# The first iteration of a seven-product down-projection: s4·b22 moved to fourth place in a PSUM bank of its own, s1·t1 to last, and the low parts of b22 loaded ahead of the last tiles of high parts

## The chip, the core and the metric

The kernel runs on one core of a Trainium2 chip. The time is the device time of one execution in microseconds; the number to predict is its median over several runs. In a profile, PE is TensorE's matmul side and PEld its weight loads, ACT is ScalarE, DVE is VectorE, POOL is GpSimd, SP is SyncE, whose queue issues nearly all DMAs here. The granted clock is the share of full speed that TensorE was allowed.

## What is computed

Two sequences of 4096 tokens with 640 channels go through a spectral block (a Fourier transform along the tokens, a block-diagonal complex MLP on the frequencies, a soft threshold, the inverse transform) and a gated FFN (640 to 1728 to 640). A gate per token mixes the two:

```python
g = sigmoid((x * gate_w).sum(-1, keepdims=True))
a = irfft2(softshrink(mlp(rfft2(x))))                   # block-diagonal MLP on 4 blocks of 160 channels
b = (gelu(x @ w_gate) * (x @ w_up)) @ w_down            # w_down: 1728 x 640
return g * a + (1 - g) * b
```

Everything is float32. The matmuls take each operand as a sum of a high part and a low part and add up three products of parts (high by high, low by high, high by low).

## The kernel before, in words

The program runs in three stretches. The first (to about 1380 us) computes the hidden layer of the FFN, with the forward transform's first stage in between, and writes the hidden layer to HBM (`hD`). The second (to about 1810 us) does the frequency MLP and the first stage of the inverse transform. The third has 32 iterations `i`: each takes the second stage of the inverse transform (`inv2`) for 256 tokens, in two groups of 128 rows called n1 and n2, and adds to it the down-projection of the same tokens (`down`).

**The down-projection** is a two by two block product done with seven block products in place of eight. Of the hidden layer, a11, a12, a21, a22 are blocks of 128 tokens by half of the 1728 rows; s1 to s4 are sums and differences of them, made by `h_s1` to `h_s4`. Of `w_down`, b11, b21, b22 and t1 to t4 are blocks or their sums and differences, 320 columns wide. The products are a11·b11, s2·t2, s3·t3, s1·t1, a12·b21, a22·t4 and s4·b22. The long dimension of a block is cut in seven pieces, `j` = 0 to 6. `rows` gives the matmuls of a product piece by piece: three for each j (high by high, low by high, high by low), and two at j = 6 where the left side is in `HALF`, so that a product has 21 or 20 matmuls of 128x128 by 128x320. `run` issues them into one PSUM bank in order of j. `h_op` splits a left side in its parts: the high part on ACT, the low part on DVE, into a tile `ho`.

**Iterations 1 to 31** interleave two products at a time (`duo`). **Iteration 0** does not, since the right sides are still being loaded: it runs a11·b11 (bank A), s2·t2 (B), then the 12 matmuls of `inv2(1)`, s3·t3 (C), s1·t1 (E), a12·b21 (added to A), a22·t4 (Dd), s4·b22 (added to E). After a product, DVE adds the bank to the staging tile `e` or, scaled by a gate, to the output tiles `uu`, u1 for group n1 and u2 for n2 (`scaled`). Between the products stand hooks 0 to 7, which issue what the next products need: in hook k of iteration 0 the entry of `SEQ` for k is split by `h_op`; hooks 1 and 2 load the hidden layer of iteration 1 (`h_load`, tile `hraw`), hook 2 also issues `inv2(1)`, hook 4 makes s3 and s2 of iteration 1 on POOL, hooks 5 to 7 split its a11, a22 and s2.

**The right sides** lie split in HBM (`wdf` for j = 0 to 6, `wdl` for the low parts of b22) and are loaded once into tiles `wx`, which stay for all 32 iterations. `wd_load(j, part)` issues on SP: part 0, both parts of b11 and t2; part 1, both parts of t3 and the low parts of t1 and b21; part 2, a tile with the low part of t4 and the high part of b22 (128x640; for j = 6 it comes with part 3), and, put off until `wd_later()`, a tile with the high parts of t1, b21 and t4 (128x960); part 3, the low parts of b22 for three j at a time (128x960), or for j = 6 alone (128x320), followed by the 128x640 tile of j = 6. The table `fin` says after which of the 64 steps of the second stretch (S = 64) each is issued; its last entry, S + 1, is issued just before iteration 0, and the two tiles of `wd_load(5, 2)` come in hook 0 of iteration 0.

**What sets the order.** The order is written out by hand: each engine and each queue takes its instructions in the order in which the program issues them. `st` puts a store off until `flush()`, which issues all that have gathered; a store waits on SP for the engine that writes its source, and what SP issues later stands behind it. The DMAs of SP use eight semaphores in turn, and before a DMA takes one, SP waits for the transfer that had it eight DMAs earlier. In the entry S + 1 the call `(flush,)` issues the last two stores of the inverse transform's first stage (`scr2<-is`, called `scr<-is` in the profile). Buffers of a tile pool go round, too: in iteration 0 one of the two `uu` tiles that `inv2(1)` writes takes the buffer of the `is` tile from which the first of these two stores reads, so that ACT's first write to it waits for that store to have landed.

Of the kernel before, what the change touches and what calls it, by code (L numbers as in the profile page):

```python
# [213 lines left out]
def spectral_mix_kernel(ctx: ExitStack, tc: tile.TileContext, a):  # L214
    nc = tc.nc
    out = a["out"]
# [10 lines left out]
    def bank():  # L227
        return psum.tile([P, 512], F32, name="bank", tag="bank")
# [13 lines left out]
    def small(shape, dt=F32, name="small"):  # L242
        return pool.tile(shape, dt, name=name, tag="small", bufs=18)
# [7 lines left out]
    def st(dst, src):  # L251
        late.append((dst, src))
# [217 lines left out]
    def run(dst, ops, first=True):  # L470
        for i, (l, r) in enumerate(ops):
            nc.tensor.matmul(dst, l, r, start=first and i == 0, stop=i == len(ops) - 1, skip_group_check=True)  # L472
            while inner and i == 1:
                inner.pop()()
# [669 lines left out]
    def h_s4(i):  # L1144
        d = HR[i]
        for k in range(2):
            nc.vector.tensor_sub(d["s2"][k], d["a12"][k], d["s2"][k])
        d["s4"] = d.pop("s2")
# [41 lines left out]
    def down(i, u, hooks):  # L1190
        b, na = c_seq[i]
        n1, n2 = toks(na)
        g1, g2 = gs[:, b, 1, n1:n1 + 1], gs[:, b, 1, n2:n2 + 1]
        u1, u2 = u[n1], u[n2]
        c1, c2 = slice(0, 320), slice(320, 640)
        acc = lambda: bank()[:, :320]

        def rows(a_, b_):
            h = HO.pop((i, a_))
            ops = []  # L1200
            for j, (hh, hl) in enumerate(h):
                wh, wl = WM[j][b_]
                ops.append([(hh, wh), (hh, wl)] if j == 6 and a_ in HALF else [(hh, wh), (hl, wh), (hh, wl)])
            return ops

        def blk(a_, b_):
            return sum(rows(a_, b_), [])

        def duo(X, x, Y, y, hook, more=False):

            n = [0, 0]
            hx, hy = rows(*x), rows(*y)
            tot = [sum(map(len, h)) for h in (hx, hy)]
            for j, (p, q) in enumerate(zip(hx, hy)):
                if j == 4:
                    hook()
                for k, op in ((0, p[0]), (0, p[1]), (1, q[0]), (0, p[2]), (1, q[-1]), *([(1, q[1])] if len(q) == 3 else ())):
                    nc.tensor.matmul((X, Y)[k], *op, start=n[k] == 0 and not (more and k), stop=n[k] == tot[k] - 1,  # L1218
                                     skip_group_check=True)
                    n[k] += 1  # L1220

        def scaled(dst, x, g):
            nc.vector.scalar_tensor_tensor(dst, x, g, dst, op0=OP.mult, op1=OP.add)
        hooks[0]()
        e = small([P, 2, 320], name="e")
        A = acc()
        if i:
            Dd = acc()
            duo(A, ("a11", "b11"), Dd, ("a22", "t4"), hooks[1])
            nc.scalar.activation(e[:, 0], A, AF.Copy)  # L1230
            hooks[2]()
            B, E = acc(), acc()
            duo(B, ("s2", "t2"), E, ("s1", "t1"), hooks[3])
            nc.vector.tensor_add(e[:, 0], B, e[:, 0])
            scaled(u2[:, c2], E, g2)
            hooks[4]()
            C = acc()
            duo(C, ("s3", "t3"), A, ("a12", "b21"), hooks[5], True)
            nc.vector.tensor_add(e[:, 1], C, e[:, 0])
            scaled(u2[:, c2], e[:, 1], g2)  # L1240
            scaled(u1[:, c1], A, g1)
        else:
            run(A, blk("a11", "b11"))
            nc.scalar.activation(e[:, 0], A, AF.Copy)
            hooks[1]()
            B = acc()
            run(B, blk("s2", "t2"))
            nc.vector.tensor_add(e[:, 0], B, e[:, 0])
            hooks[2]()
            C = acc()  # L1250
            run(C, blk("s3", "t3"))
            nc.vector.tensor_add(e[:, 1], C, e[:, 0])
            hooks[3]()
            E = acc()
            run(E, blk("s1", "t1"))
            for x in (E, e[:, 1]):
                scaled(u2[:, c2], x, g2)
            hooks[4]()
            run(A, blk("a12", "b21"), first=False)
            scaled(u1[:, c1], A, g1)  # L1260
            hooks[5]()
            Dd = acc()
            run(Dd, blk("a22", "t4"))
        nc.vector.tensor_add(e[:, 1], Dd, e[:, 1])
        scaled(u2[:, c1], e[:, 1], g2)
        st(out[b, n2], u2)
        hooks[6]()
        run(E, blk("s4", "b22"), first=False)
        nc.vector.tensor_add(e[:, 0], E, e[:, 0])
        scaled(u1[:, c2], e[:, 0], g1)  # L1270
        st(out[b, n1], u1)
        hooks[7]()
# [113 lines left out]
    for i, key in enumerate(keys):  # L1386
# [16 lines left out]
        for j, t in enumerate(quads):  # L1403
            def hook(k):
                for f in slots.get((i, 7 * j + k), ()):
                    f()
# [27 lines left out]
    S = len(steps)  # L1434
# [3 lines left out]
    for ch in range(1, 2 * NCH):  # L1438
        b, c = chunks[ch]
# [6 lines left out]
    def events(i, j):  # L1446
        for f, *args in todo.get((i, j), []):
            f(*args)
    wl = lambda part, *js: [(wd_load, j, part) for j in js]
# [9 lines left out]
           S - 2: [(h_load, 0, 0), *wl(1, 2), (h_load, 0, 1)],  # L1459
           S - 1: [(c_split, 0), (h_op, 0, "a11"), *wl(1, 3, 4, 5), *wl(0, 6), (h_s3, 0, nc.gpsimd), (c_load, 1)],  # L1460
           S: [(h_s2, 0), (h_op, 0, "s2"), (c_split, 1)],
           S + 1: [*wl(1, 6), (flush,), *wl(2, 6), (wd_later,), *wl(2, 4), (wd_later,), *wl(3, 0, 3, 6), (h_s1, 0)]}
    for i in range(S + 2):
        events(i, 0)
        flush()
# [16 lines left out]
        if 0 <= i - 1 < S:  # L1482
            b, c, n = steps[i - 1]
# [5 lines left out]
            f(*args)  # L1489


    SEQ = dict(enumerate(("s3", "s1", "a12", "a22", "s4")))
    DUO = {0: "s1", 2: "s3", 3: "a12", 4: "s4"}
    for i in range(len(c_seq)):
        n = i + 1 if i + 1 < len(c_seq) else None
# [3 lines left out]
        def step(k):  # L1499
            def f():  # L1500
# [7 lines left out]
                if k == (1 if i else 0):  # L1508
                    h_s4(i)
                op = (SEQ if i == 0 else DUO).get(k)  # L1510
                if op:
                    h_op(i, op)
                if n is not None:
# [16 lines left out]
                    if k == 7:  # L1530
                        h_op(n, "s2")
            return f
        down(i, uu, [step(k) for k in range(8)])
    flush()

# [20 lines left out]
```

## Time and profile before

| | |
|---|---|
| median of 3 runs | 2548.75 us (2548.2 to 2549.05) |
| the profiled execution: its own time, its span | 2548.73 us, 2547.0 us |
| granted clock over the span | 0.998 |
| PE busy | 2533.7 us, 99% of the span |
| DVE, ACT, POOL busy | 2053.1, 1491.7, 372.4 us |
| HBM read and written | 300.55 MB and 179.64 MB |
| matmuls of the down-projection: iteration 0 and the last 20 (line 472); the rest (line 1218) | 764; 3844 |

A row of the timeline has the start in us from the span's start, the duration, engine, line, operation, output and inputs, the count of merged instructions, and in brackets the idle time of the engine before it with what ended it. A row of the waits has the total, the number of times and the longest. A row of the chain has start, duration and what ran or was under way. A row of the windows has the stretch and its length, the busy time and the count of instructions of PE, PEld, DVE, ACT and POOL in it, TensorE's granted clock, the busy share of the DMA engines and the GB/s that they moved.

### The profile page before, as it was taken

To read this page: it belongs to the slowest core of one execution; us is meant where nothing else is said; L and a number is where in the kernel's file an instruction comes from. 1 tells how busy PE (TensorE), PEld (TensorE's weight loads), DVE (VectorE), ACT (ScalarE), POOL (GpSimd) and SP (SyncE) were. 2 spreads that over 40 slices of the span, in tenths; PEclk is the share of its full clock that TensorE was granted. 3 is DMA by queue.
4 is the path that set the end of the run, shared out by engine and by line. 5 is a ranking of instruction groups with operands and counts; after the bars stand their busy time and mean duration, and the time that the engine had idled before them with its cause. 6 is when DMAs were issued, how large, how long until landed. Compare 5 with 4: busy or idle time off the path is not lost.

```text
span 2547.0 us, 54577 instructions
## 1 busy us (share of the span) xinstructions
PE 2533.7 (99%) x20317; PEld 2529.6 (99%) x20317; DVE 2053.1 (81%) x4214; ACT 1491.7 (59%) x3489; POOL 372.4 (15%) x379
## 2 busy tenths in 40 slices
PE   9999999999999999999999999999899999999999
PEld 9999999999999999999999999999899999999999
DVE  7778767777777766776667788888899999899998
ACT  5555555666665655565556787777544444444443
POOL 0000000000000000000003111111133333333332
PEclk9999999999999999999999999999999999999999
DMA  6565647676767667776677455548744444444432
GB/s 222 188 226 187 220 169 230 201 243 209 223 207 249 199 221 231 224 227 214 213 226 228 127 153 156 155 145 266 267 145 152 156 146 143 137 152 156 153 131 100
DMA packets 345311, 483.77 MB, mean 190 GB/s; under 512 B 24717, under 2 KB 220941, under 8 KB 345045
## 3 DMA queue, kind: packets, MB, share of 16 engines
q1 hardware_dynamic: 330212, 438.47, 53.8%
q0 software_dynamic: 14832, 41.82, 4.6%
q8 instruction: 160, 2.62, 0.4%
q14 instruction: 107, 0.87, 0.1%
HBM read 300.55 MB, written 179.64 MB: 189 GB/s over the span
## 4 chain that ended last, share of the span: by engine, by line
PE 98%; DMA 1%; DVE 1%; ACT 0%; issue 0%; SPq 0%; DVEq 0%; ACTq 0%
PE bank L472 56%; PE bank L1218 22%; PE bank L295 14%; PE bank L798 3%; PE bank L632 1%; PE bank L879 1%; PE bank L880 1%; DMA wx<-wdf 1%; DMA s<-scr 0%; PE bank L881 0%; PE bank L1310 0%; DVE xd L430 0%; DVE xo L279 0%; DVE h L543 0%; DVE w L279 0%
## 5 line engine op out<-in xcount | busy, mean ns | idle before, releaser
L472 PE MATMUL bank<-xo,w 128*128 128x256 f32 x11736 | 1360.4, 277 | 0.3 <-ACT u L498 0.3
L472 PEld LDWEIGHTS bank<-xo,w 128*128 128x128 f32 x11736 | 1351.8, 188 | 0.8 <-ACT u L498 0.7
L1218 PE MATMUL bank<-wx,ho 128*128 128x320 f32 x3844 | 560.8, 306 | 0.0
L1218 PEld LDWEIGHTS bank<-wx,ho 128*128 128x128 f32 x3844 | 557.2, 188 | 0.0
L498 ACT ACTIVATE u<-bank 128x256 f32<-128x256 f32 x408 | 156.6, 384 | 255.9 <-PE bank L472 250.0
L279 DVE TENSOR_TENSOR ho<-hraw,ho 128x640 fp32r<-128x640 f32 (+3 forms) x384 | 272.1, 749 | 22.6 <-ACT ho L276 19.7
L276 ACT ACTIVATE ho<-hraw 128x640 fp32r<-128x640 f32 x320 | 167.1, 571 | 98.2 <-PE bank L1218 65.8
L498 ACT ACTIVATE p<-bank 128x256 f32<-128x256 f32 x204 | 78.6, 385 | 151.0 <-PE bank L472 63.4
L279 DVE TENSOR_TENSOR xo<-xraw,xo 128x512 fp32r<-128x512 f32 x209 | 143.3, 686 | 24.2 <-ACT xo L276 23.7
L531 DVE TENSOR_TENSOR u<-bank,u 128x256 f32<-128x256 f32 x204 | 86.0, 422 | 89.6 <-ACT u L498 86.8
L279 DVE TENSOR_TENSOR xs<-xr,xs 64x640 fp32r<-64x640 f32 x128 | 105.0, 820 | 57.5 <-ACT xs L276 55.5
L295 PE MATMUL bank<-wm,h 128*128 128x320 f32 (+1 forms) x792 | 137.6, 309 | 0.0
L276 ACT ACTIVATE xo<-xraw 128x512 fp32r<-128x512 f32 x208 | 130.4, 627 | 7.1 <-DMA xraw<-in_xT_dram 5.2
L540 DVE TENSOR_TENSOR u<-bank,u 128x256 f32<-128x256 f32 x204 | 85.6, 419 | 60.4 <-PE bank L472 59.5
L634 DVE TENSOR_TENSOR as<-bank,as 64x320 f32<-64x320 f32 x256 | 113.9, 484 | 24.9 <-ACT as L633 23.8
L472 PE MATMUL bank<-wx,ho 128*128 128x320 f32 x764 | 119.5, 312 | 6.6 <-DMA wx<-wdf 6.6
L472 PEld LDWEIGHTS bank<-wx,ho 128*128 128x128 f32 x764 | 114.7, 192 | 7.1 <-issue 5.2
L295 PEld LDWEIGHTS bank<-wm,h 128*128 128x128 f32 (+1 forms) x792 | 117.9, 185 | 1.3
L585 POOL MEMSET h<- 64x512 f32 x16 | 8.4, 523 | 748.2 <-PE bank L632 408.4
L514 DVE TENSOR_TENSOR p<-bank,p 128x256 f32<-128x256 f32 x204 | 86.6, 425 | 37.1 <-PE bank L472 32.7
L276 ACT ACTIVATE ho<-hs 128x640 fp32r<-128x640 f32 (+1 forms) x128 | 68.9, 570 | 68.0 <-DVE ho L279 50.8
L633 ACT ACTIVATE as<-bank 64x320 f32<-64x320 f32 x256 | 96.8, 427 | 16.4 <-PE bank L632 13.9
(167 smaller groups left out, 3658.9 us busy)
## 6 DMA issues: line engine op xcount, KB each, us to landing
xo<-xD SPq DMA_DIRECT2D x124, 512.0 KB
xraw<-in_xT_dram SPq DMA_DIRECT2D x225, 256.0 KB
hD<-h SPq DMA_DIRECT2D x224, 256.0 KB
hraw<-hD SPq DMA_DIRECT2D x128, 320.0 KB
xD<-xo POOLq DMA_DIRECT2D x64, 512.0 KB, 4.1
sc<-scr SPq DMA_DIRECT2D x65, 320.0 KB
xr<-in_x_dram SPq DMA_DIRECT2D x64, 320.0 KB
scr<-as SPq DMA_DIRECT2D x64, 320.0 KB
```

What stands on the lines that cost most here:

```text
L276: nc.scalar.activation(dst, src, AF.Copy, scale=scale)
L279: eng.tensor_sub(dst, src, hi.bitcast(F32))
L295: nc.tensor.matmul(dst, l, r, start=i == 0, stop=i == len(ops) - 1)
L472: nc.tensor.matmul(dst, l, r, start=first and i == 0, stop=i == len(ops) - 1, skip_group_check=True)
L498: copy = lambda d, s_: nc.scalar.activation(d, s_, AF.Copy)
L514: nc.vector.tensor_add(p1, A, p1)
L531: nc.vector.tensor_add(u4, C, u4)
L540: nc.vector.tensor_add(u2, C, u2)
L633: nc.scalar.activation(stg[hi, cs], pa[lo, :320], AF.Copy)
L634: nc.vector.tensor_add(stg[hi, cs], pa[hi, :320], stg[hi, cs])
L798: nc.tensor.matmul(pz[:, kp * P:(kp + 1) * P], SC[b, c, kp][:, o:o + P], ft, start=True, stop=True)
L1218: nc.tensor.matmul((X, Y)[k], *op, start=n[k] == 0 and not (more and k), stop=n[k] == tot[k] - 1, skip_group_check=True)
```

## The change

Iteration 0 gets a new order: s4·b22 runs fourth, into a bank F of its own, and s1·t1 runs last, into E. `SEQ` follows, so hook 1 splits s4 and hook 4 splits s1. Since E no longer gathers two products, DVE adds it to u1 and to u2 apart, and `e` is added to the outputs as soon as s3·t3 is done. In the entry S + 1 of `fin`, part 3 (`wdl`, and the last 128x640 tile) is issued right after part 1 of j = 6, ahead of the stores of `flush` and of part 2 of j = 6 and 4.

```diff
             nc.vector.tensor_add(e[:, 1], C, e[:, 0])
+            for u_, c_, x, g in ((u2, c2, 1, g2), (u2, c1, 1, g2), (u1, c2, 0, g1)):
+                scaled(u_[:, c_], e[:, x], g)
             hooks[3]()
-            E = acc()
-            run(E, blk("s1", "t1"))
-            for x in (E, e[:, 1]):
-                scaled(u2[:, c2], x, g2)
+            F = acc()
+            run(F, blk("s4", "b22"))
+            scaled(u1[:, c2], F, g1)
             hooks[4]()
             run(A, blk("a12", "b21"), first=False)
             scaled(u1[:, c1], A, g1)
             hooks[5]()
             Dd = acc()
             run(Dd, blk("a22", "t4"))
+            scaled(u2[:, c1], Dd, g2)
+            hooks[6]()
+            E = acc()
+            run(E, blk("s1", "t1"))
+            scaled(u1[:, c2], E, g1)
+            st(out[b, n1], u1)
+            scaled(u2[:, c2], E, g2)
+            st(out[b, n2], u2)
+            hooks[7]()
+            return
...
-           S + 1: [*wl(1, 6), (flush,), *wl(2, 6), (wd_later,), *wl(2, 4), (wd_later,), *wl(3, 0, 3, 6), (h_s1, 0)]}
+           S + 1: [*wl(1, 6), *wl(3, 0, 3, 6), (flush,), *wl(2, 6), (wd_later,), *wl(2, 4), (wd_later,), (h_s1, 0)]}
...
-    SEQ = dict(enumerate(("s3", "s1", "a12", "a22", "s4")))
+    SEQ = dict(enumerate(("s3", "s4", "a12", "a22", "s1")))
```

On SP, between the second stretch and iteration 0, the one piece of the difference (`wdf_111` is j = 6, `wdf_109` j = 4, `wdf_110` j = 5; the first row is part 1 of j = 6, the last two are issued in hook 0):

```order
 L1068 DMA wx<-wdf_111 128x1280
+L1068 DMA wx<-wdl 128x960 x2
+L1068 DMA wx<-wdl 128x320
+L1068 DMA wx<-wdf_111 128x640
 L256 DMA scr_1_71<-is 16x16x320 x2
 L1068 DMA wx<-wdf_111 128x960
 L1068 DMA wx<-wdf_109 128x640
 L1068 DMA wx<-wdf_109 128x960
-L1068 DMA wx<-wdl 128x960 x2
-L1068 DMA wx<-wdl 128x320
-L1068 DMA wx<-wdf_111 128x640
 L1068 DMA wx<-wdf_110 128x640
```

Four loads move from behind the two stores and three loads to ahead of them.

On PE, the fourth product of iteration 0 from j = 3 on, before (s1·t1 into E; `wx_26620`, `wx_26633`, `wx_26616` are the 128x960 tiles of j = 4, 5 and 6, the other tiles are part 1):

```order
L472 MATMUL bank_26779<-wx_26620,ho_26668 128x320 x2
L472 MATMUL bank_26779<-wx_26490,ho_26668 128x320
L472 MATMUL bank_26779<-wx_26633,ho_26669 128x320
L472 MATMUL bank_26779<-wx_26633,ho_26670 128x320
L472 MATMUL bank_26779<-wx_26492,ho_26669 128x320
L472 MATMUL bank_26779<-wx_26616,ho_26669 128x320
```

and now (s4·b22 into F; `wx_26625`, `wx_26631` are the 128x640 tiles of j = 4 and 5, `wx_26616` the low parts for j = 3 to 5, `wx_26618` both parts for j = 6):

```order
L472 MATMUL bank_26783<-wx_26616,ho_26668 128x320
L472 MATMUL bank_26783<-wx_26625,ho_26668 128x320 x2
L472 MATMUL bank_26783<-wx_26616,ho_26668 128x320
L472 MATMUL bank_26783<-wx_26631,ho_26669 128x320
L472 MATMUL bank_26783<-wx_26631,ho_26670 128x320
L472 MATMUL bank_26783<-wx_26616,ho_26669 128x320
L472 MATMUL bank_26783<-wx_26618,ho_26669 128x320 x2
```

The fourth product no longer reads the 128x960 tiles of high parts; of j = 4 and 5 it reads the 128x640 tiles, each of which is issued just ahead of the 128x960 tile of the same j.

## The prediction

> **What bounds the kernel now.** I read the waits of PE first, then PE's timeline where iteration 0 stands, then SP's timeline and the DMA windows there, to see what PE waits for. PE is busy for 99% of the span. Its whole list of waits (total, times, longest) has one row that concerns this change:
>
> ```profile
> PE bank L472 <- DMA wx<-wdf: 6.6, 2, 4.9
> ```
>
> Both pauses lie in iteration 0 (start, duration, idle time before it in brackets):
>
> ```profile
> 1809.89 6.32 PE L472 MATMUL bank<-wx,ho 128*128 128x320 f32 x42
> 1816.05 1.90 PE L295 MATMUL bank<-s2s,v 128*128 128x320 f32 x12
> 1817.79 5.04 PE L472 MATMUL bank<-wx,ho 128*128 128x320 f32 x33
> 1824.49 0.70 PE L472 MATMUL bank<-wx,ho 128*128 128x320 f32 x3 [1.66 <-DMA wx<-wdf]
> 1830.13 12.45 PE L472 MATMUL bank<-wx,ho 128*128 128x320 f32 x66 [4.93 <-DMA wx<-wdf]
> 1842.41 17.87 PE L1218 MATMUL bank<-wx,ho 128*128 128x320 f32 x122
> ```
>
> The 33 matmuls are the 21 of s3·t3 and the first 12 of s1·t1, j = 0 to 3. Then PE waits 1.66 us for the high part of t1 at j = 4, does its three matmuls, and waits 4.93 us for j = 5. The last row gives the undisturbed pace, 17.87 / 122 = 0.1465 us a matmul. At that pace the 66 would take 9.67 us; they took 12.45, so 2.78 us are lost once more. The windows (stretch, length, PE busy, the other engines, clock, DMA share, GB/s) show why:
>
> ```profile
> 1822.21:1825.62 3.41, 1.32 (x8) 0.81 (x6) 2.19 (x6) 0.23 (x1) 0.00 (x0) 1.00 1.03 413
> 1825.63:1829.04 3.41, 0.00 (x0) 0.00 (x0) 0.00 (x0) 0.00 (x0) 0.00 (x0) 0.50 1.04 409
> 1829.04:1832.45 3.41, 2.32 (x9) 2.35 (x10) 0.34 (x1) 1.08 (x2) 0.35 (x1) 0.50 1.05 379
> 1832.45:1835.86 3.41, 3.41 (x14) 3.41 (x14) 3.37 (x4) 0.07 (x1) 3.41 (x3) 0.50 0.14 46
> 1835.87:1839.00 3.13, 3.13 (x23) 3.13 (x23) 3.07 (x5) 1.05 (x2) 1.57 (x2) 1.00 0.00 0
> ```
>
> The clock fell to half at 1825.63, at the end of a stretch in which PE was busy for 1.32 of 3.41 us, and came back 10.24 us later, after a stretch busy throughout. So the stall costs 1.66 + 4.93 + 2.78 = 9.37 us. That is all that this change can win.
>
> Why the tiles are late stands in SP's timeline, in its row of waits on DVE, and in the chain (start, duration from issue to landing):
>
> ```profile
> 1804.19 1.26 SPq L256 DMA_DIRECT2D scr<-is  x2
> 1806.17 0.33 SPq L1068 DMA_DIRECT2D wx<-wdf  x1
> 1814.62 1.21 SPq L256 DMA_DIRECT2D scr<-is  x2
> 1815.87 1.84 SPq L1068 DMA_DIRECT2D wx<-wdf  x3
> 1817.77 2.24 SPq L1068 DMA_DIRECT2D wx<-wdl  x3
> 1820.06 2.79 SPq L1068 DMA_DIRECT2D wx<-wdf  x3
> ...
> SPq L256 <- DVE is L976: 68.2, 13, 8.2
> ...
> 1803.46 8.88 DMA s<-scr
> 1815.87 6.59 DMA wx<-wdf
> 1822.53 7.46 DMA wx<-wdf
> ```
>
> From 1806.5 to 1814.6 SP issues nothing: it stands at the flush, 8.2 us, until DVE has written the last `is`. Nine loads queue behind. Meanwhile the DMA engines use up what was issued before:
>
> ```profile
> 1810.00:1812.00 2.00, 2.00 (x16) 2.00 (x15) 1.25 (x3) 1.17 (x3) 0.00 (x0) 1.00 1.05 396
> 1812.00:1814.00 2.00, 2.00 (x16) 2.00 (x15) 1.63 (x4) 1.77 (x6) 0.00 (x0) 1.00 0.97 380
> 1814.00:1816.00 2.00, 2.00 (x16) 2.00 (x15) 2.00 (x6) 1.74 (x5) 0.00 (x0) 1.00 0.18 65
> 1816.00:1818.00 2.00, 2.00 (x16) 1.94 (x15) 2.00 (x5) 0.91 (x3) 0.00 (x0) 1.00 1.06 312
> 1818.00:1820.00 2.00, 2.00 (x15) 2.00 (x15) 2.00 (x5) 2.00 (x5) 0.00 (x0) 1.00 0.90 241
> 1820.00:1822.00 2.00, 2.00 (x16) 2.00 (x15) 2.00 (x5) 2.00 (x5) 0.00 (x0) 1.00 0.94 326
> 1822.00:1824.00 2.00, 0.83 (x6) 0.58 (x4) 1.94 (x6) 0.44 (x2) 0.00 (x0) 1.00 1.01 414
> ```
>
> A full queue moves 380 to 414 GB/s; I take 400, or 0.4 MB a us. From 1814 the queue runs dry, 65 GB/s, and the next three rows refill slowly. Against 400 the four rows miss 335 + 88 + 159 + 74 = 656 GB/s over 2 us, 1.31 MB, or 3.3 us.
>
> **The change part by part: the loads.** A 128x960 tile is 0.492 MB, a 128x640 tile or a store 0.328 MB, the short `wdl` load 0.164 MB, the 128x1280 tile 0.655 MB. I reckon SP's transfers as moved in the order of their issue, and need one anchor: the second `s<-scr` landed at 1803.46 + 8.88 = 1812.34, and behind it stood two stores and the 128x1280 tile of 1806.17, 1.31 MB, 3.28 us: it lands at 1815.6. As a check on the kernel before: the two stores and the nine loads behind it, to the tile of 1822.53, are 4.26 MB, 10.65 us, so 1826.3 with a full queue; it landed at 1822.53 + 7.46 = 1829.99. The 3.7 us between are the 3.3 us of the dry queue, near enough.
>
> Now the four moved loads, 1.475 MB, come ahead of the flush. Two things could hold them on SP, a buffer and a semaphore. By the order with its waits they wait for four transfers only, the last being the first `s<-scr`, which the second one's 1812.34 bounds; so they are issued before the queue runs out at 1815.6, and the flush is not later than its 1814.62. The queue stays full. With 1815.6 and 0.4 MB a us: the four loads have landed at 1819.3, the stores at 1820.9, the 128x960 tile of j = 6 at 1822.2, the 128x640 tile of j = 4 at 1823.0, its 128x960 tile at 1824.2, the 128x640 tile of j = 5 at 1825.0, its 128x960 tile at 1826.3.
>
> **The products.** All up to s3·t3 stays, so the fourth product starts at 1817.79 + 21 x 0.1465 = 1820.87. It is now s4·b22. It wants the low parts from 1821.2 (there since 1819.3), the 128x640 tile of j = 4 at 1820.87 + 12 x 0.1465 = 1822.63 and that of j = 5 three matmuls later. These land at 1823.0 and 1825.0: stalls of 0.4 and 1.6 us, 2.0 in all. With 380 or 420 GB/s the second is there at 1825.5 or 1824.6, so 1.5 to 2.5 us. a12·b21 then starts at 1825.8 and wants the last tile, of j = 5, at 1828.0; it is there at 1826.3. s1·t1, which made both waits, comes 20 + 20 matmuls later still.
>
> The Trainium skill speaks against this reckoning: "DMA: Bandwidth & Descriptors", section Specifications, gives a limit of about 358 GB/s from HBM for a core. By it the stall would be 3.0 us and the sum 1 us higher; the rows above, up to 414 GB/s, do not agree, and I stay with them.
>
> **The engines.** These rows of ACT, DVE and POOL stand around it:
>
> ```profile
> 1817.87 1.78 ACT L1185 ACTIVATE uu<-bank,gs 128x320 f32<-128x320 f32 x4 [1.09 <-PE bank L295]
> 1819.52 1.99 ACT L276 ACTIVATE ho<-hraw 128x640 fp32r<-128x640 f32 x4
> 1830.88 0.74 ACT L276 ACTIVATE ho<-hraw 128x640 fp32r<-128x640 f32 x1 [8.43 <-DMA hraw<-hD]
> 1817.02 2.22 DVE L279 TENSOR_TENSOR ho<-hraw,ho 128x640 fp32r<-128x640 f32 x4
> 1821.39 1.33 DVE L279 TENSOR_TENSOR ho<-hraw,ho 128x640 fp32r<-128x640 f32 x3
> 1832.11 0.55 DVE L1223 SCALAR_TENSOR_TENSOR uu<-bank,gs,uu 128x320 f32<-128x320 f32 x1 [7.61 <-PE bank L472]
> 1834.56 2.89 POOL L1136 TENSOR_TENSOR hs<-hraw 128x640 f32<-128x640 f32 x2
> ```
>
> Splitting s4 in place of s1 is one small DVE subtraction more (a third where 2.22 has four): done near 1819.4, wanted at 1820.9. The three additions of `e` after s3·t3 cost 3 x 0.55 us, and DVE has one instruction more than before; both lie under the stall and under 8 us of products, and would cost 1 to 2 us only if DVE had to feed a12 or a22 at once. The bank F is free without a wait that the order shows. The second `uu` tile on ACT waits for the first store, due at 1820.1: then three of its four writes (1.34 us), the two high parts of a12 (1.0) and DVE's 1.33 end at 1823.8; PE wants a12 at 1825.8, and would at 1823.8 without the stall. That store's cover is thus 2.0 us. Iteration 1 wants its first left sides at 1835.0, 7.4 us sooner than 1842.41; `hraw`, 1830.88 before, lands 3.7 us sooner with the queue and is split while a22·t4 and s1·t1 run, and POOL's sums, which end at 1837.45 before the change, are wanted only 41 matmuls, 6 us, after that start. I put all of this at nothing.
>
> **The sum**, on the profiled execution's 2548.73 us: less 1.66, 4.93 and 2.78, plus 2.0: 2541.4 us, with 1.5 to 2.5 us of stall 2540.9 to 2541.9. The median of the runs, 2548.75, is the same to 0.02 us, so nothing is added for it.
>
> **The rivals.**
>
> A shorter stall. If the 128x640 tiles land a us or more earlier than reckoned, 0 to 1 us is left: 2539.4 to 2540.4. The slow refill has no row that says how early loads behave under stores; against it stands the steady 400.
>
> The clock falls all the same. The row of 1822.21 shows a fall after 39% busy in 3.41 us; 2.0 us of stall in the same length leaves 41%, if one such stretch holds all of it, and more if two share it. No row shows where between 39% and a busy stretch the limit lies. Once fallen, the rows show the clock back only after a stretch of 3.41 us wholly busy, so 3.4 to 6.8 us at half pace cost 1.7 to 3.4 us: 2543.1 to 2544.8.
>
> The Trainium skill, "TensorE: Matmul & The Clock Gate", section "What's actually happening", has half rate return after at least one idle window of about 3.4 us. By that rule the stall leaves the clock alone, and the sum stays. The trace agrees in the length but not in "idle": the longest pause before the fall was 1.66 us, then 0.44 us of the next.
>
> The queue refills no better. If the slow rows 1816 to 1822 came from the stores among the loads and not from the dry queue, and the gap at 1814 reappears later, the last tile still lands at 1829.99 and the 128x640 tile of j = 5, now just ahead of it, at 1828.8. Then s4·b22 waits 5.7 us in place of 6.6, with the same clock: 2547.8. For it speaks that two stores lie in the slow rows; against, that stores moved at 380 to 396 GB/s at 1810 to 1814.
>
> Slower: the store holds ACT. The two stores now have 1.475 MB of loads ahead of them, and ACT's `uu` waits for the first. Were its packets put off until the queue is empty, all loads and the 1.83 MB of `hraw` first, it would land near 1830.9; a12 would be ready 3.7 us later, at 1834.6, which makes 8.8 us of waiting after the 2.0, and with 2.78 of clock the total is 4.2 us over before: 2552.9. It decides from a landing at about 1826.7. Against it: the stores of 1804.19 stood in a full queue too, and by the row of 1814 nothing was left in it.
>
> **How the numbers follow.** A measurement of this kernel can tell about 0.2%, 5.1 us, from no change. The forecast, a short stall at full clock, 2541.4: 0.48. Shorter stall: 0.08. Clock falls: 0.30, of which 0.19 below 2543.65 (the 0.2% line). Queue no better: 0.10. Store holds ACT: 0.04, about half beyond the line on the slow side, with other mishaps. Faster 0.48 + 0.08 + 0.19 = 0.75; slower 0.03; same 0.22. The range leaves out the last two cases: from 2539.0, where nothing of the 9.37 us is left, with the spread of the runs, to 2545.5, above the fallen clock.
>
> **What would show it.** Right: SP issues three `wx<-wdl` between 1807 and 1813; no window from 1814 to 1822 below 350 GB/s; PE idle about 2 us near 1823 to 1825, on `wx<-wdf`, none before a12·b21 or s1·t1; 66 or so matmuls at 0.1465 us and PEclk 1.00. Wrong: `wx<-wdl` issued after 1814.6; a pause of PE that ACT or DVE ends; a row of half clock; a pause before iteration 1.

## The result and the profile after

The changed kernel takes 2542.65 us, the median of 10 runs (2540.69 to 2543.53); the kernel before, on the same chip, 2548.44 us (10 runs, 2547.04 to 2549.73). The ratio is 0.9976, 95% interval 0.9966 to 0.9985. The profiled execution of after took 2543.41 us, with a span of 2541.6.

PE's timeline of after around iteration 0 (start, duration, idle time before it in brackets):

```profile
1810.23 6.31 PE L472 MATMUL bank<-wx,ho 128*128 128x320 f32 x42
1818.12 4.97 PE L472 MATMUL bank<-wx,ho 128*128 128x320 f32 x33
1823.86 0.70 PE L472 MATMUL bank<-wx,ho 128*128 128x320 f32 x3 [0.77 <-DMA wx<-wdf]
1825.93 11.33 PE L472 MATMUL bank<-wx,ho 128*128 128x320 f32 x66 [1.37 <-DMA wx<-wdf]
1837.10 13.10 PE L1218 MATMUL bank<-wx,ho 128*128 128x320 f32 x89
```

The two pauses are now in s4·b22, 0.77 and 1.37 us where before had 1.66 and 4.93. The next 66 matmuls take 11.33 us, which is 1.66 more than 66 x 0.1465. From the first matmul of iteration 0 to the first of iteration 1 are 1837.10 - 1810.23 = 26.87 us; in before these are 1842.41 - 1809.89 = 32.52. This stretch, **iteration 0** below, is what the profiles are compared by: it holds the pauses that the change is about, and not what differs between runs ahead of it. Behind it, from the first matmul of iteration 1 to the end of the span, nearly all profiles of this document have 704.4 to 704.6 us; the two exceptions are named where they come up.

SP's timeline of after:

```profile
1807.60 3.65 SPq L1068 DMA_DIRECT2D wx<-wdl  x3
1811.79 0.32 SPq L1068 DMA_DIRECT2D wx<-wdf  x1
1814.85 1.50 SPq L256 DMA_DIRECT2D scr<-is  x2
1816.45 3.52 SPq L1068 DMA_DIRECT2D wx<-wdf  x5
```

The DMA windows of after there (the last number is GB/s, the third from the end the clock):

```profile
1814.00:1816.00 2.00, 2.00 (x16) 2.00 (x15) 2.00 (x5) 1.67 (x5) 0.00 (x0) 1.00 1.02 413
1816.00:1818.00 2.00, 2.00 (x16) 2.00 (x15) 2.00 (x5) 1.00 (x2) 0.00 (x0) 1.00 1.03 406
1818.00:1820.00 2.00, 2.00 (x15) 2.00 (x15) 1.94 (x6) 0.58 (x2) 0.00 (x0) 1.00 1.07 403
1820.00:1822.00 2.00, 2.00 (x16) 2.00 (x15) 0.94 (x3) 0.90 (x3) 0.00 (x0) 1.00 1.02 411
```

The flush still waits for DVE, until 1814.85, but four loads have been issued ahead of it, and the four windows that had 65, 312, 241 and 326 GB/s now have 403 to 413.

The windows of the clock in after:

```profile
1822.35:1825.76 3.41, 1.44 (x9) 0.92 (x7) 3.31 (x8) 2.91 (x7) 0.00 (x0) 1.00 1.03 407
1825.77:1829.18 3.41, 3.25 (x12) 3.28 (x13) 3.35 (x8) 1.04 (x2) 0.08 (x1) 0.50 1.07 390
1829.18:1832.59 3.41, 3.41 (x25) 3.41 (x24) 1.49 (x3) 1.05 (x2) 3.41 (x3) 1.00 0.22 73
```

One stretch of 3.41 us holds nearly all of both pauses, 1.97 of 2.14 us, with PE busy for 1.44 of it, 42%; the clock is at half for the 3.41 us behind it.

ACT's timeline of after shows how the store holds it up:

```profile
1821.10 1.37 ACT L1185 ACTIVATE uu<-bank,gs 128x320 f32<-128x320 f32 x3 [2.44 <-DMA scr<-is]
```

ACT stands still for 2.44 us, until the store has landed. No row of PE names ACT or DVE here.

### The profile page after: what moved, and what is told of

Its sections match the earlier page's. It is cut to its first block, busy times and chain, and to the rows that moved or that the text cites. A ratio compares the mean times of both kernels' runs of the same rounds, so it can differ in the third digit from the quotient of the medians.

```text
span 2541.6 us, 54579 instructions
## 1 busy us (share of the span) xinstructions
PE 2533.0 (100%) x20317; PEld 2529.0 (100%) x20317; DVE 2053.7 (81%) x4215; ACT 1491.8 (59%) x3489; POOL 372.3 (15%) x379
## 4 chain that ended last, share of the span: by engine, by line
PE 97%; DVE 1%; DMA 1%; issue 0%; ACT 0%; DVEq 0%
PE bank L472 55%; PE bank L1218 22%; PE bank L295 14%; PE bank L798 3%; PE bank L632 1%; DMA wx<-wdf 1%; PE bank L879 1%; PE bank L880 1%; DMA wx<-wdl 0%; PE bank L881 0%; PE bank L1321 0%; DVE xd L430 0%; DVE xo L279 0%; DVE wl L728 0%; DVE h L543 0%
```

## The experiments

The theory: the tiles are late because the DMA queue runs dry at the flush, and the clock falls in the stretch that holds PE's pauses. The main rivals: the new order of products makes the gain by itself; the order among the loads does, and the flush is no matter; the store's hold on ACT reaches PE. Each kernel was timed beside before on its chip; after itself was timed twice more, as after_again and after_third.

| kernel | median (runs), us | ratio to before, 95% | iteration 0 in its profile, us |
|---|---|---|---|
| before | 2548.44, 2547.87, 2548.23, 2547.39 | | 32.52 |
| after | 2542.65 (10) | 0.9976 [0.9966, 0.9985] | 26.87 |
| loads_only | 2544.23 (11) | 0.9986 [0.9978, 0.9995] | 27.52 |
| order_only | 2545.38 (11) | 0.9988 [0.9979, 0.9996] | 28.12 |
| behind_flush | 2547.73 (11) | 0.9997 [0.9988, 1.0006] | 30.01 |
| filled | 2540.92 (7) | 0.9974 [0.9963, 0.9985] | 25.19 |
| after_again | 2542.24 (10) | 0.9979 [0.9970, 0.9988] | 25.21 |
| small_ahead | 2540.19 (6) | 0.9969 [0.9958, 0.9981] | 22.75 |
| high_ahead | 2542.10 (7) | 0.9973 [0.9962, 0.9984] | 23.07 |
| a12_early | 2541.09 (11) | 0.9977 [0.9968, 0.9986] | 24.81 |
| after_third | 2541.08 (11) | 0.9977 [0.9968, 0.9986] | 24.70 |
| filled_again | 2541.41 (11) | 0.9977 [0.9969, 0.9986] | 25.06 |
| small_ahead_again | 2539.55 (5) | 0.9969 [0.9956, 0.9981] | 23.01 |
| small_ahead_a12 | 2538.49 (5) | 0.9966 [0.9954, 0.9979] | 23.80 |

The four medians of before belong to the four groups in the table's order: after; loads_only to filled; after_again to a12_early; after_third to small_ahead_a12.

### The loads alone

The kernel before with after's place of the loads; the order of products stays that of before:

```diff
-           S + 1: [*wl(1, 6), (flush,), *wl(2, 6), (wd_later,), *wl(2, 4), (wd_later,), *wl(3, 0, 3, 6), (h_s1, 0)]}
+           S + 1: [*wl(1, 6), *wl(3, 0, 3, 6), (flush,), *wl(2, 6), (wd_later,), *wl(2, 4), (wd_later,), (h_s1, 0)]}
```

> The loads of after (three wx<-wdl and one wx<-wdf ahead of the flush) with the order of products of before (s1*t1 fourth, s4*b22 last). Queue theory (a tile's landing is set by the bytes ahead of it in a queue that stays full): s1*t1 wants the 128x960 tiles of j = 4 and 5 near 1823.0 and 0.44 us behind; after's trace has them landing near 1825.0 and 1827.0, so two pauses of 2.0 and 1.5 us, 3.5 in all in place of 6.6. With the clock at half for 3.4 to 6.8 us besides: 2548.7 - 9.4 + 3.5 + (1.7 to 3.4) = 2544.5 to 2546.2; with the clock left alone 2542.8. Rival, that the whole gain comes from the order of products: 2548.5, as before. Rival, that it all comes from the loads: 2542.6, as after.

PE's timeline of loads_only:

```profile
1824.30 0.69 PE L472 MATMUL bank<-wx,ho 128*128 128x320 f32 x3 [1.54 <-DMA wx<-wdf]
1826.36 11.19 PE L472 MATMUL bank<-wx,ho 128*128 128x320 f32 x66 [1.37 <-DMA wx<-wdf]
1837.39 0.90 PE L1218 MATMUL bank<-wx,ho 128*128 128x320 f32 x5
1838.61 17.49 PE L1218 MATMUL bank<-wx,ho 128*128 128x320 f32 x119 [0.32 <-DVE ho L279]
```

Pauses of 1.54 and 1.37 us in place of 1.66 and 4.93, and a clock at half for 3.41 us. The median, 2544.23, is 0.3 us below the range expected with a fall of the clock. So the loads win 3.6 us of the median by themselves, and the rival that the whole gain comes from the order of products is out. The rival that it all comes from the loads is not excluded by the medians, since the two intervals overlap from 0.9978 to 0.9985; against it stand the pauses, 2.91 us in all where after has 2.14, and the next kernel. The last row has a pause that after does not have: in iteration 1 PE waits 0.32 us for a split by DVE. From iteration 1 to the end this profile has 705.1 us.

### The order of products alone

```diff
-           S + 1: [*wl(1, 6), *wl(3, 0, 3, 6), (flush,), *wl(2, 6), (wd_later,), *wl(2, 4), (wd_later,), (h_s1, 0)]}
+           S + 1: [*wl(1, 6), (flush,), *wl(2, 6), (wd_later,), *wl(2, 4), (wd_later,), *wl(3, 0, 3, 6), (h_s1, 0)]}
```

> The order of products of after with the loads of before (three wx<-wdl behind the flush, last but three in the queue). Queue theory: s4*b22 then waits for wx<-wdl (landing 1825.7 to 1827.3 in before) and for the 128x640 tile of j = 5 (1828.8 in before), wanted at 1823.1: 5.7 us of pause in one or several pieces in place of 6.6, and the half clock as in before: 2547.5 to 2548.5. Rival, that the order of products alone makes the gain: 2541 to 2543.

PE's timeline of order_only:

```profile
1817.72 3.53 PE L472 MATMUL bank<-wx,ho 128*128 128x320 f32 x23
1824.32 2.77 PE L472 MATMUL bank<-wx,ho 128*128 128x320 f32 x13 [3.06 <-DMA wx<-wdl]
1827.59 10.53 PE L472 MATMUL bank<-wx,ho 128*128 128x320 f32 x66 [0.50 <-DMA wx<-wdf]
1837.95 18.08 PE L1218 MATMUL bank<-wx,ho 128*128 128x320 f32 x124
```

My number missed: 2545.38, about 2 us below the range, though still 3 us above after. The waits are the ones expected, but they are 3.56 us in all and not 5.7: the first `wx<-wdl` is there at 1824.3, where before's had 1825.7. Of this 1.4 us the flush itself gives 0.6 (it issues at 1813.99, in before at 1814.62); the rest is open. And with matmuls between the two pauses PE is busy for 2.90 of the 3.41 us behind the fall of the clock, so it is at half for 3.41 us, not 10.24. The order alone is thus worth 2.5 us of the median (its interval ends at 0.9996, just short of no change) and is no mere preparation for the loads. One part wins 3.6, the other 2.5, both 5.8 to 6.3.

### The moved loads right behind the flush

```diff
-           S + 1: [*wl(1, 6), *wl(3, 0, 3, 6), (flush,), *wl(2, 6), (wd_later,), *wl(2, 4), (wd_later,), (h_s1, 0)]}
+           S + 1: [*wl(1, 6), (flush,), *wl(3, 0, 3, 6), *wl(2, 6), (wd_later,), *wl(2, 4), (wd_later,), (h_s1, 0)]}
```

> After with one edit: the four moved loads stand right behind the flush, in the same order among all other loads, so that the queue has nothing between about 1814 and 1815.6, as in before. Theory of the dry queue: the window 1814 to 1816 is again below 150 GB/s, the 128x640 tile of j = 5 lands near 1828.8, s4*b22 waits about 5.7 us, the clock falls: 2547.5 to 2548.5. Rival, that the order among the loads is what matters and the flush is not: 2542.0 to 2543.5, as after.

In this profile iteration 0 begins at 1812.61, 2.7 us later than in before. Its DMA windows:

```profile
1816.00:1818.00 2.00, 2.00 (x15) 2.00 (x15) 2.00 (x6) 2.00 (x6) 0.00 (x0) 1.00 0.39 158
1818.00:1820.00 2.00, 2.00 (x16) 2.00 (x15) 2.00 (x5) 0.67 (x2) 0.00 (x0) 1.00 0.68 188
1820.00:1822.00 2.00, 2.00 (x15) 1.93 (x14) 1.97 (x5) 1.98 (x6) 0.00 (x0) 1.00 1.04 296
1822.00:1824.00 2.00, 2.00 (x15) 1.84 (x13) 1.97 (x6) 2.00 (x5) 0.00 (x0) 1.00 1.02 353
```

And PE's timeline of behind_flush:

```profile
1812.61 6.32 PE L472 MATMUL bank<-wx,ho 128*128 128x320 f32 x42
1828.79 1.17 PE L472 MATMUL bank<-wx,ho 128*128 128x320 f32 x3 [2.70 <-DMA wx<-wdf]
1830.85 11.93 PE L472 MATMUL bank<-wx,ho 128*128 128x320 f32 x66 [0.90 <-DMA wx<-wdf]
1842.62 17.64 PE L1218 MATMUL bank<-wx,ho 128*128 128x320 f32 x121
```

The dry spot is back, and the gain is gone by the median: 2547.73, where before has 2547.87. By iteration 0 more than half of it is gone: 30.01 us, between after's 26.87 and before's 32.52. From after this kernel differs only in four loads that stand on the other side of the flush, in the same order among all loads, so the rival "order among the loads" can't be the cause of after's gain. That order does count, though: order_only has the same four loads behind the three others of the entry S + 1 in place of ahead of them, and is 2.3 us shorter by the median (the intervals overlap, 0.9979 to 0.9996 and 0.9988 to 1.0006) and 1.9 us shorter in iteration 0. In both kernels the windows right behind the dry spot refill slowly, as in before; why is open. The pauses are 3.84 us, with a short one of 0.24 on `wx<-wdl`. The matmuls between them are slowed by the half clock, and the row of j = 5 starts at 1830.85, 18.2 us behind the start of iteration 0, where before's rows, undisturbed, put it 13.2 behind: 5.1 us late of the 5.7 expected. The clock is at half for 6.83 us.

### PE kept busy in the pauses

14 matmuls more, into a bank that a22·t4 later starts anew; what is computed stays:

```diff
-            F = acc()
-            run(F, blk("s4", "b22"))
+            F, Dd = acc(), acc()
+            x, y = HO[i, "s4"][0][0], WM[0]["b11"][0]
+            for j, r in enumerate(rows("s4", "b22")):
+                for k in range({4: 5, 5: 9}.get(j, 0)):
+                    nc.tensor.matmul(Dd, x, y, start=True, stop=True, skip_group_check=True)
+                for k, (l, m) in enumerate(r):
+                    nc.tensor.matmul(F, l, m, start=j == 0 and k == 0, stop=j == 6 and k == 1, skip_group_check=True)
...
-            Dd = acc()
```

> After with 14 matmuls more in s4*b22, 5 ahead of its row j = 4 and 9 ahead of j = 5; they write into the bank that a22*t4 uses later and starts anew, so what is computed stays. They stand in the two pauses (0.77 and 1.37 us in the profile of after), so PE is busy there. Clock theory (the runs of after, 2540.7 to 2543.5, differ by whether the clock falls after these pauses): the clock stays at 1.00, the 14 matmuls take the place of 2.05 us of pause, and all runs lie at 2541.0 to 2541.9. Rival, that the spread has another source: the same spread, median 2542.6. If the 14 matmuls do not fit in the pauses, up to 1 us more than 2541.4.

PE's timeline of filled, where L1260 is the added line:

```profile
1822.13 0.89 PE L1260 MATMUL bank<-wx,ho 128*128 128x320 f32 x5
1822.87 0.72 PE L1262 MATMUL bank<-wx,ho 128*128 128x320 f32 x3
1823.43 1.48 PE L1260 MATMUL bank<-wx,ho 128*128 128x320 f32 x9
```

No pause is left and the clock stays at 1.00. Six of seven runs lie at 2540.56 to 2541.64, one at 2544.41 with a mean clock of 1.000, so that no fall made it long. Beside after on one chip, though:

> After with the 14 filling matmuls, beside after on one chip. Clock theory: no run at a mean clock of 0.999 or below, median 2540.6 to 2541.4, 0.5 to 2 us below after_third. Rival: no difference from after_third.

> After itself, unchanged, timed beside the three kernels that follow. 2540.7 to 2543.5 as before; by the clock theory its runs fall into two groups, near 2541 without a fall of the clock and near 2543 with one.

> After itself beside filled_again and the two kernels with the small tiles ahead. Median 2541.5 to 2543, runs from 2540.7 to 2546; where a profile shows the stretch of 3.41 us that holds the pauses busy 42% or less, the clock falls and the run is 1.5 to 2 us longer; where it is busy 60% or more, it does not.

filled_again has 2541.41, after_third 2541.08: no gain, and one of its 11 runs has a mean clock of 0.999. The reason is in the profiles of after_again and after_third, where the clock stays up behind PE's pauses as they are. The stretch ahead of the long pause and the one that holds it, of after_again:

```profile
1820.72:1824.13 3.41, 3.38 (x24) 3.10 (x22) 3.16 (x8) 3.26 (x8) 0.00 (x0) 1.00 1.03 398
1824.13:1827.54 3.41, 2.08 (x15) 1.86 (x14) 3.30 (x8) 0.89 (x2) 0.00 (x0) 1.00 1.04 395
```

and of after_third:

```profile
1821.06:1824.47 3.41, 3.33 (x23) 3.08 (x23) 2.86 (x7) 2.89 (x7) 0.00 (x0) 1.00 1.03 412
1824.47:1827.88 3.41, 2.05 (x13) 1.82 (x14) 3.31 (x8) 1.26 (x4) 0.00 (x0) 1.00 1.04 404
```

The long pause is there, 1.33 and 1.36 us, and PE is busy for 61% and 60% of the stretch that holds it. But the short one, 0.77 us in after, is all but gone: the first rows leave PE idle for 0.03 and 0.08 us. In both the next stretch is at 1.00, and iteration 0 is 25.21 and 24.70 us, not 26.87. So what decides between these three profiles is first the short pause, that is, how soon the 128x640 tile of j = 4 lands against PE's need of it; whether the same two pauses would leave the clock up if the stretches began elsewhere, no profile shows.

How often the clock falls in after's runs can only be bounded. All profiles here with a fall in iteration 0 have a mean clock of 0.998 or 0.999, all without it 1.000; by that, at most 8 of after's 31 runs had a fall (2542.36 to 2545.85) and at least 23 had none. It is a bound, since the clock also falls behind PE's last matmuls: in after_again it is at half for the last 2.3 us of the span, which by itself nearly makes a 0.999. So the clock theory holds for the profiles, and fell as an explanation of the whole spread: runs without a fall reach 2544.47.

### The store's hold on ACT

```diff
-                if (i, k) == (0, 2):
-                    ahead.update(inv2(1))
                 if k in (0, 5):
                     flush()
                 if k == (1 if i else 0):
                     h_s4(i)
                 op = (SEQ if i == 0 else DUO).get(k)
                 if op:
                     h_op(i, op)
+                if (i, k) == (0, 2):
+                    ahead.update(inv2(1))
```

> After, with the split of a12 written ahead of the second pair of uu tiles, so that ACT makes it before it stands 2.44 us for the store scr<-is. Prediction's step: the store's hold on ACT is covered by the products, so the time stays that of after within 0.3 us (median 2541.5 to 2543.0), and the pauses in s4*b22 stay. Rival, that the hold reaches PE by a way that the trace does not name: 1 to 2.4 us less.

The median is 2541.09, 1.15 us below after_again's 2542.24 on the same chip. That lies in the rival's range, but the intervals overlap almost wholly, after_third without this edit has the same ratio, and iteration 0 of 24.81 us stands between after_third's 24.70 and after_again's 25.21. PE still waits, on `wx` alone:

```profile
1822.85 0.72 PE L472 MATMUL bank<-wx,ho 128*128 128x320 f32 x3 [0.19 <-DMA wx<-wdf]
1824.90 9.85 PE L472 MATMUL bank<-wx,ho 128*128 128x320 f32 x66 [1.33 <-DMA wx<-wdf]
```

So the hold is covered as far as the trace tells. A gain of some tenths can't be told from none.

### More tiles ahead of the flush

small_ahead moves both 128x640 tiles that s4·b22 waits for ahead of the flush too:

```diff
-           S + 1: [*wl(1, 6), *wl(3, 0, 3, 6), (flush,), *wl(2, 6), (wd_later,), *wl(2, 4), (wd_later,), (h_s1, 0)]}
+           S + 1: [*wl(1, 6), *wl(3, 0, 3, 6), *wl(2, 4, 5, 6), (flush,), (wd_later,), (h_s1, 0)]}
...
-                if (i, k) == (0, 0):
-                    wd_load(5, 2)
-                    wd_later()
```

> After, with the two 128x640 tiles of j = 4 and 5 moved ahead of the flush as well, and the 128x960 tiles in the order 4, 5, 6 behind the stores. Queue theory, with 0.4 MB a us from the tile of after that lands at 1816.7: the 128x640 tiles are there near 1821.0 and 1821.8, 1.9 and 1.6 us before s4*b22 wants them, so its two pauses (2.14 us) go; a12*b21 starts 2.1 us sooner and wants the 128x960 tiles from 1826.0 on; they land near 1824.7, 1825.9 and 1827.1, so 0 to 0.5 us of pause there. Without a pause of 1 us the clock stays up: 2543.4 - 2.1 - 1.7 + (0 to 0.5) = 2539.6 to 2540.1, median of the runs 2539.5 to 2540.5. Rival, that the pause only moves into a12*b21 (the same bytes are ahead of the last tile): 1 us or more there, 2541 to 2543.

> Both 128x640 tiles of j = 4 and 5 ahead of the flush, beside after on one chip. Queue theory: no pause of PE on wx in iteration 0, median 2539.0 to 2540.5, 1.5 to 3 us below after_third. Rival, that the runs at 2541 to 2542 of the first trial are its usual time: 0 to 1 us below after_third.

PE's timeline of small_ahead:

```profile
1810.00 6.32 PE L472 MATMUL bank<-wx,ho 128*128 128x320 f32 x42
1817.89 15.02 PE L472 MATMUL bank<-wx,ho 128*128 128x320 f32 x102
1832.75 18.07 PE L1218 MATMUL bank<-wx,ho 128*128 128x320 f32 x124
```

From s3·t3 on, all 102 matmuls of iteration 0 run in one piece, 0.147 us each. 2540.19 and 2539.55: the second is 1.5 us below after_third on one chip, with runs of 2537.94 to 2540.41 against 2539.85 to 2543.59; the intervals of the two ratios overlap, so the size is rough. That the pauses are gone is plain in both profiles. The pause does not move into a12·b21. That the bytes ahead of the last tile are the same is no harm, since that tile is wanted later.

high_ahead does the like for the order of products of before: the 128x640 and 128x960 tiles of j = 4 to 6 ahead of the flush, the low parts behind it. The difference is against before:

```diff
-           S + 1: [*wl(1, 6), (flush,), *wl(2, 6), (wd_later,), *wl(2, 4), (wd_later,), *wl(3, 0, 3, 6), (h_s1, 0)]}
+           S + 1: [*wl(1, 6), *wl(2, 6), (wd_later,), *wl(2, 4), (wd_later,), *wl(2, 5), (wd_later,), (flush,), *wl(3, 0, 3, 6), (h_s1, 0)]}
...
-                if (i, k) == (0, 0):
-                    wd_load(5, 2)
-                    wd_later()
```

> The order of products of before (s1*t1 fourth, s4*b22 last), with all 128x640 and 128x960 tiles of j = 4 to 6 ahead of the flush and the three wx<-wdl and their 128x640 tile behind it. Queue theory: only what stands ahead of the flush counts, not which product comes fourth. The 128x960 tiles of j = 4 and 5 land near 1820.8 and 1822.8, wanted at 1823.0 and 1823.4; wx<-wdl and its 128x640 tile near 1827, wanted after 1829. No pause, clock at 1.00: 2539.4 to 2540.5. Rival, that s4*b22 fourth is needed for the gain: 2542.5 or more, as loads_only (2544.2).

PE's timeline of high_ahead:

```profile
1810.65 6.32 PE L472 MATMUL bank<-wx,ho 128*128 128x320 f32 x42
1818.54 15.34 PE L472 MATMUL bank<-wx,ho 128*128 128x320 f32 x102
1833.72 0.90 PE L1218 MATMUL bank<-wx,ho 128*128 128x320 f32 x5
1834.86 17.49 PE L1218 MATMUL bank<-wx,ho 128*128 128x320 f32 x119 [0.25 <-DVE ho L279]
```

The mechanism is confirmed: no pause in iteration 0 with s1·t1 fourth either. The time is not: three runs lie at 2538.36 to 2540.52, four at 2542.10 to 2542.32, all at a mean clock of 1.000, and the median is near after_again's. As in loads_only, PE waits a little for a split by DVE in iteration 1, 0.25 us, and from there to the end the profile has 705.0 us. The profile is of one of the short runs, so what the four others lose stays open.

The last kernel adds the earlier splits to small_ahead (a12 as in a12_early, and the step of a22 ahead of the additions of `e`):

> small_ahead with the splits of a12 and a22 written earlier (a12 ahead of the second pair of uu tiles, a22 ahead of the additions of e). small_ahead shows no pause on ho in iteration 0, so the time should be that of small_ahead_again within 0.4 us; a gain of 1 us would mean a wait on ACT or DVE that the profile of small_ahead did not show.

Its five runs are 2538.34 to 2539.69, median 2538.49, the lowest of all, 8.9 us below before on its chip. That is 1.1 us under small_ahead_again, more than the 0.4 expected, but the two ratios' intervals overlap almost wholly, and its profile has a pause of 0.76 us on a split by DVE that small_ahead's two profiles do not have. All five runs are shorter than the shortest of after_third's 11, 2539.85. That it beats before and after is shown; that it beats small_ahead is not.

## Why the prediction was right, and where not

**The dry queue: right.** SP issues the `wx<-wdl` loads at 1807.60 to 1811.25, within the 1807 to 1813 named, and all windows of after from 1814 to 1822 are above 350 GB/s (after_again has one of 347). behind_flush undoes this alone and loses the gain of the median. The reckoning took the slow refill behind the dry spot as part of it, and after bears that out, but why the refill is slow no run shows.

**The stall: right in place and cause, its sum partly by luck.** In the profiled execution it is 0.77 + 1.37 = 2.14 us against 0.4 + 1.6 = 2.0, in s4·b22, for `wx<-wdf`, with none ahead of a12·b21 or s1·t1. In the other two profiles of after it is 1.36 and 1.43 us, below the range of 1.5 to 2.5: the long pause is steady, 1.33 to 1.37 us, and the short one goes from 0.03 to 0.77. The Trainium skill, "DMA: Bandwidth & Descriptors", section Specifications, has a limit of about 358 GB/s for a core, half of what it gives for a stack, and by an estimate from that the stall would have been 3.0; the rows of 403 to 413 GB/s speak against it here as before.

**The engines at nothing: right.** The store was later than reckoned: ACT goes on at 1821.10, not 1820.1. a12's split ends at 1824.5, where 1823.8 was said; PE began a12·b21 only behind the last pause, and no row waits for it. One of the three profiles of after, after_again, has a pause of 0.30 us on a split by DVE. It lies behind the first matmul of s3·t3, so ahead of the instruction more that s4 costs DVE. There the load `s<-scr` came later (ACT waits 1.38 us for it, in after 0.73), and DVE begins the split of s3 at 1817.82, in after at 1817.22. small_ahead_a12's 0.76 us stand at the same place.

**The clock: the forecast's case is the usual one, not that of the profiled run.** The profiled execution went the way of the rival "the clock falls all the same": 1.66 us at half clock, 2543.41 us, in its range of 2543.1 to 2544.8. In the other two profiles, and by the mean clock in at least 23 of 31 runs, it stays. The chance that I gave the rival, 0.30, stands beside at most 8 of 31. The fork is not the one named there, whether one stretch holds the whole stall: in all three profiles one stretch holds nearly all of it, and what differs is the short pause, 0.77 us or next to nothing. One step failed: that the clock comes back only after a stretch wholly busy. It came back after 95% here, and after 85% in order_only. By the Trainium skill, "TensorE: Matmul & The Clock Gate", section "What's actually happening", an idle window brings half rate; the trace disagrees, since a stretch with PE busy for 42% and no pause over 1.37 us was enough.

**The size.** In iteration 0 the forecast is 32.52 - 9.37 + 2.0 = 25.15 us; the three profiles show 26.87 (with the fall), 25.21 and 24.70. small_ahead's 22.75 and 23.01, without a pause, say that before lost 9.5 to 9.8 us here, not 9.37. A part of the difference is in before's three matmuls between its pauses, which took 0.70 us where the pace gives 0.44; the rest is not resolved. The median, 2542.65, is 1.25 above the 2541.4, and the gains of the three groups, 5.8, 6.0 and 6.3 us, are 1.0 to 1.5 us short of 7.3. Falls in at most a quarter of the runs, at 1.7 us each, explain at most 0.4 of that; for the rest there is only one profile of before to set against its runs of 2544.64 to 2551.65, so it stays open.

## What to carry to other kernels

Where a queue's engine stands at a store that waits for a compute engine, look at what the DMA engines still have to do behind it: loads issued ahead of that wait, up to the point where they no longer run dry, were worth more here (5 us of the median between behind_flush and after) than the choice between the two orders that were tried behind it (2.3 us). Put ahead of the wait what is wanted first: the version that did so to the end removed all pauses for loads. Changes of a few microseconds in thousands are judged best by a stretch between two fixed instructions in the profiles, since the total carries the spread of all that runs ahead; but it takes more than one profile of a kernel, since after's own three differ by 2.2 us in iteration 0.

## What the runs showed of the hardware

**The clock goes by stretches of 3.41 us and the share of PE in them.** The changes of the clock stand whole numbers of such stretches apart: in after, from its return at 1829.18 to its fall behind PE's last matmuls at 2539.15 are 709.97 us, 208 times 3.413. In a profile without a fall in iteration 0 the stretches are counted back from that last fall. In iteration 0 the clock fell behind stretches busy for 27% (behind_flush), 29% (loads_only), 39% (before, order_only) and 42% (after), and did not behind 60% (after_third), 61% (after_again) and, in order_only, 71%. It came back after 85% (order_only), 86% (loads_only) and 95% (after), and did not after 68% (before, behind_flush). Windows of order_only:

```profile
1818.82:1822.23 3.41, 2.43 (x17) 2.17 (x15) 3.38 (x8) 2.97 (x7) 0.00 (x0) 1.00 0.99 363
1822.23:1825.64 3.41, 1.32 (x9) 1.33 (x10) 3.31 (x8) 0.00 (x0) 0.00 (x0) 1.00 1.02 405
1825.65:1829.05 3.40, 2.90 (x11) 2.52 (x10) 0.02 (x1) 0.00 (x0) 0.00 (x0) 0.50 1.04 403
```

and of behind_flush:

```profile
1828.58:1831.98 3.40, 2.30 (x7) 1.93 (x8) 0.43 (x2) 0.00 (x0) 0.00 (x0) 0.50 1.04 403
```

The end of the span narrows it: behind the last matmuls of after_third the clock stayed up after a stretch busy for 45%, and fell only after the next, at 2541.27, with PE idle:

```profile
2534.45:2537.86 3.41, 1.54 (x11) 1.27 (x9) 2.07 (x5) 0.00 (x0) 0.00 (x0) 1.00 0.24 96
2537.87:2541.27 3.40, 0.00 (x0) 0.00 (x0) 0.00 (x0) 0.00 (x0) 0.00 (x0) 1.00 0.24 96
```

So in these profiles the clock falls after 42% and less and stays after 45% and more, and a short pause can pass from one side to the other: without its 0.77 us the stretch of after would be busy for 2.21 of 3.41 us, 65% by this reckoning. In after it cost itself and 1.7 us at half clock besides.

**The time ahead of iteration 0 is not fixed.** Its first matmul stands at 1808.67 (small_ahead_again) to 1812.61 us (behind_flush). One source shows in a window at full clock in which PE is never idle, of before:

```profile
400.00:420.00 20.00, 20.00 (x179) 20.00 (x178) 17.15 (x51) 12.68 (x35) 0.00 (x0) 1.00 0.72 219
```

and of behind_flush:

```profile
400.00:420.00 20.00, 20.00 (x172) 20.00 (x172) 16.29 (x48) 11.91 (x32) 0.00 (x0) 1.00 0.69 204
```

172 matmuls in place of 179 in the same 20 us; what slows them is open.
